# Attention decode backward: scores as 512-column matmuls, and other row splits for nine of the gradient stores

## The chip, the cores and the metric

The kernel runs on one core of a Trainium2 chip. The metric is device time in microseconds (us) of one launch, as the median of several executions. Lower is better.

## The reference

One query row attends to 8192 keys for each of 2 x 32 = 64 heads, and the gradients of q, k and v are wanted as well as the output. All tensors are bf16.

```python
B, H, Sq, Sk, D = 2, 32, 1, 8192, 128

def _fwd_reference(q, k, v):
    scale = q.shape[-1] ** -0.5
    scores = jnp.einsum("bhqd,bhkd->bhqk", q, k) * scale
    p = _softmax(scores, axis=-1)
    return jnp.einsum("bhqk,bhkd->bhqd", p, v)

def reference(q, k, v, grad_out):
    _out, _vjp = jax.vjp(_f, q, k, v)      # _f is _fwd_reference
    return (_out, *_vjp(grad_out))         # out, dq, dk, dv
```

For one head this is: s = K q; p = softmax(s * scale); out = p V; dp = V g (g is the row of grad_out); dS = p * (dp - sum(p * dp)) * scale; dq = dS K; dk = dS times q as an outer product; dv = p times g as an outer product. Each head reads 2 MB of K and 2 MB of V and writes 2 MB of dk and 2 MB of dv, so 537 MB cross between device memory and the core in one launch.

## The kernel before

A head's K and V are each one tile `kvt` of 128 partitions x 64 rows x 128 columns: partition p holds the 64 consecutive keys from 64p on, which are 16 KB in one piece in memory. There are twelve such tiles (`NTILE`), used in turn. dk is written over K in its tile and dv over V, and the tile is stored from there. The tile of a new head is thus free only when the store of the old gradient has landed.

The program is one loop over slots `g`. A slot takes one chunk of 16 key rows per partition; a head has eight slots, four for K (w = 0) and four for V (w = 1). `at(r0)` and `within(r0)` pick the head that has reached a given slot of its own schedule, so a head's later stages stand beside the first stages of the next heads. `pin` keeps every instruction in program order on its engine. The stages of a head are:

- `load` (L98): DMAs issued by SP, six heads ahead. SP works in order and waits until the tile's last store has landed.
- `transpose_chunk`: 16 TensorE transposes into `tp` (L184), copied by ScalarE to `ev` (L186).
- `score_chunk` (L195), one slot later: 16 matmuls, each with a 128x128 block of `ev` as weights and q (or g) as the one moving column. The scores land in the layout [partition, key row], in `sw` for K and `dpw` for V.
- `max_part`, `max_all`, `max_spread`, `expo`: VectorE's row maximum (L207), a maximum over the partitions by way of TensorE (L211, L218), ScalarE's exponential (L238), and the weights `E_pad` (L247) for the matmuls with V.
- `normalise_p`, `weigh`, `normalise_ds`: sums over partitions by fp32 matmuls with ones (L282), then `dS_pad` and the factors `pair` of the outer products.
- `acc` (L339): out and dq, as matmuls with 64 weight columns and 512 moving columns, in two column groups of TensorE; `pick` and `join` (L356, L362, L376) take the wanted blocks out of them.
- `broadcast` (L168, L177): q or g on all partitions.
- `outer` (L394): VectorE writes dk or dv over the tile, and the last chunk's store is issued: by GpSimd (L412), or for the last head in four pieces by SP.

Eight dk stores, those of the heads in `SPREAD`, are cut by `by_rows` (L87) into a DMA of 126 partitions and one of 2. At the start q's first `FIRST` = 6 rows come by a GpSimd DMA (L110) after a reset of that queue's cursor, and the other 58 by SP (L114).

```python
FIRST = 6
SPREAD = range(4, 60, 7)
...
            if w == 0 and i in SPREAD:
                by_rows(store_eng, dst, h.tile[w], (P - 2, 2))
```

Of the kernel before, what the change touches and what calls it, by code (L numbers as in the profile page):

```python
# [11 lines left out]
BF16 = mybir.dt.bfloat16  # L12
F32 = mybir.dt.float32

CH = 16
QT = 4
CW = 64
NG = 2
NTILE = 12
FIRST = 6  # L20
SPREAD = range(4, 60, 7)


@with_exitstack
def kernel(
# [50 lines left out]
    heads = [Head() for _ in range(BH)]  # L76

    def slot_of(i, w):

        n = 2 * i + w  # L80
        return n if n < NTILE else slot_of(i - NTILE // 2, 1 - w)

    def by_rows(eng, dst, src, rows):

        p = 0
        for m in rows:
            pin(eng.dma_start(out=dst[p : p + m], in_=src[p : p + m], max_dma_last_dim=NT * D))  # L87
            p += m

    def load(i, w, pieces=(NCH,)):  # L90
        h = heads[i]
        t = kvp.tile([P, NT, D], BF16, tag=f"kv{slot_of(i, w)}", name="kvt")
        h.tile[w] = t
        src = (v_v if w else k_v)[i]
        c = 0
        for m in pieces:
            n0, n1 = c * CH, (c + m) * CH
            pin(load_eng.dma_start(out=t[:, n0:n1, :], in_=src[:, n0:n1, :]))  # L98
            c += m
# [4 lines left out]
    for w, a in enumerate((q, grad_out)):  # L104
        rows = a.rearrange("b h s d -> (b h s) d")
        r0 = FIRST if w == 0 else 0
        if r0:
# [3 lines left out]
                    out=qd_nat[:r0, w, :], in_=rows[:r0], max_dma_last_dim=D  # L111
# [4 lines left out]
    load(0, 1)  # L116
    for j in range(1, min(NTILE // 2, BH)):
        load(j, 0)
# [17 lines left out]
    nc.vector.memset(E_pad[:], 0.0)  # L136
    nc.vector.memset(dS_pad[:], 0.0)

    qdT = const.tile([P, 2, BH], BF16)
    for w in range(2):  # L140
        tps = ps_m.tile([P, BH], BF16, tag=f"acc{w}", name="tps")
        nc.tensor.transpose(tps[:], qd_nat[:BH, w, :], ident_bf[:BH, :BH])
        nc.vector.tensor_copy(out=qdT[:, w, :], in_=tps[:])

    dqT = const.tile([P, BH], BF16)
    oT = const.tile([P, BH], BF16)

    def begin_s(i):

        h = heads[i]  # L150
        sw = ps_sdp.tile([P, NT + P + 1], F32, tag="s", name="sw")
        h.s = sw[:, 0:NT]
        h.mT = sw[0:1, NT : NT + P]
        h.mb = sw[:, NT + P :]

    def begin_dp(i):

        h = heads[i]
        dpw = ps_sdp.tile([P, NT + 2 + D], F32, tag="dp", name="dpw")
        h.dp = dpw[:, 0:NT]  # L160
        h.lsum = dpw[:, NT : NT + 2]
        h.qbp = dpw[:, NT + 2 :]

    def broadcast(i, w):

        h = heads[i]
        pin(
            nc.tensor.matmul(  # L168
                h.qbp,
                lhsT=qdT[:, w, i : i + 1].to_broadcast([P, P]),  # L170
                rhs=ident_bf[:],
                start=True,
                stop=True,
            )
        )
        h.qb[w] = small.tile([P, D], BF16, tag=f"qb{w}", name="qb")
        pin(nc.vector.tensor_copy(out=h.qb[w][:], in_=h.qbp))  # L177
# [9 lines left out]
        return ev  # L187

    def score_chunk(i, c, ev):
        h = heads[i]  # L190
        w, c = divmod(c, NCH)
        dst = h.dp if w else h.s
        for t in range(CH):
            pin(
                nc.tensor.matmul(  # L195
                    dst[:, c * CH + t : c * CH + t + 1],
                    lhsT=ev[:, t, :],
                    rhs=qdT[:, w, i : i + 1],
                    start=True,
                    stop=True,  # L200
                )
            )
# [125 lines left out]
    def acc(i, w, c):  # L328
# [59 lines left out]
    def outer(i, w, c, ends):  # L388

        h = heads[i]  # L390
        n0 = c * CH
        shape = [P, CH, D // 2, 2]
        pin(
            nc.vector.tensor_tensor(  # L394
                out=h.tile[w][:, n0 : n0 + CH, :].rearrange("p n (e t) -> p n e t", t=2),
                in0=h.qb[w][:]
                .rearrange("p (e t) -> p e t", t=2)
                .unsqueeze(1)
                .to_broadcast(shape),
                in1=h.pair[w][:, n0 : n0 + CH, :].unsqueeze(2).to_broadcast(shape),  # L400
                op=ALU.mult,
            )
        )
        if c + 1 in ends:
            at = ends.index(c + 1)
            b0, b1 = (ends[at - 1] if at else 0) * CH, (c + 1) * CH
            dst = (dv_v if w else dk_v)[i]
            if w == 0 and i in SPREAD:
                by_rows(store_eng, dst, h.tile[w], (P - 2, 2))
            else:  # L410
                eng = load_eng if len(ends) > 1 else store_eng
                pin(eng.dma_start(out=dst[:, b0:b1, :], in_=h.tile[w][:, b0:b1, :]))  # L412
# [6 lines left out]
    last = list(range(1, NCH + 1))  # L419
    AHEAD = NTILE // 2  # L420

    prev = None
    for g in range(SL * BH + O0 + NCH + 4 - SL):
        now = [(g // SL - b, g % SL + b * SL) for b in range(4)]
        now = [(i, r) for i, r in now if 0 <= i < BH]

        def at(r0):

            return next((i for i, r in now if r == r0), None)

# [12 lines left out]
        ev = None  # L443
        if g < SL * BH:
            i, r = divmod(g, SL)
            if r == 0:
                begin_s(i)
            if r == 3:
                begin_dp(i)
                broadcast(i, 1)  # L450
            if r == 6:
                broadcast(i, 0)
            ev = transpose_chunk(i, r)
        if (i := at(A1 + NCH + 2)) is not None:
            join(i, 1)
        if (i := at(A0 + NCH + 2)) is not None:
            join(i, 0)
        if x := within(A1):
            acc(x[0], 1, x[1])
        if x := within(A0):  # L460
            acc(x[0], 0, x[1])
        if (i := at(NCH + 2)) is not None:
            max_spread(i)
            expo(i)
        if prev is not None:
            score_chunk(*prev)
        prev = (g // SL, g % SL, ev) if ev is not None else None

        if (i := at(NCH)) is not None:
            max_part(i)  # L470
        if (i := at(NCH + 1)) is not None:
            max_all(i)
        if (i := at(NCH + 3)) is not None:
            normalise_p(i)
        if (i := at(SL)) is not None:
            weigh(i)
        if (i := at(SL + 1)) is not None:
            normalise_ds(i)
        if (i := at(A1 + NCH)) is not None:
            pick(i, 1)  # L480
        if (i := at(A0 + NCH)) is not None:
            pick(i, 0)

    for w, (src, dst) in enumerate(((dqT, out_1), (oT, out_0))):
        tps = ps_m.tile([BH, P], BF16, tag=f"acc{w}", name="tps")
# [34 lines left out]
```

## Time and profile before

| what | value |
|---|---|
| median of 12 runs | 1286.44 us (1284.68 to 1289.83) |
| the profiled execution, its own time | 1287.36 us |
| its span, first to last instruction | 1285.6 us |
| TensorE busy / its weight loads | 1128.3 us (88%) / 857.9 us |
| VectorE, ScalarE, GpSimd busy | 935.7, 975.1, 76.0 us |
| mean granted TensorE clock | 0.955 |
| DMA: bytes, mean rate | 539.68 MB, 420 GB/s |
| DMA: share of 16 engines' span | 49.9% SP's queue, 48.7% GpSimd's queue, 0.7% instruction fetch |

The span is what the profile sees; 1287.36 - 1285.6 = 1.8 us lie around it. "Share of 16 engines' span" says how long the packets of a queue took, summed over the 16 DMA engines of the core. A compute engine's busy time overlaps the others', and matmuls are pipelined, so a busy share is not a share of the work. A launch spans 64 heads, so one head has 1285.6 / 64 = 20.1 us, and one slot 2.51 us.

### The profile page before, as it was taken

The numbers are of one execution on the slowest core, as the hardware profiler recorded it, in microseconds if no ns is written. First come the engines' busy times: TensorE is split into PE (matmuls) and PEld (weight loads), VectorE is DVE, ScalarE is ACT, GpSimd is POOL, SyncE is SP. The second block draws the span as 40 slices with busy tenths as digits, with TensorE's granted clock in tenths as the row PEclk, the third lists the DMA queues.
The fourth block names the chain that finished last, engine by engine and source line by source line (L and its number), as shares of the span: only waits on it lengthen the run. The fifth ranks groups of instructions, "written<-read, shape, count | busy, mean of one in ns | idle before, by whom it ended". The sixth has DMA issues, their size and how long they took to land.

```text
span 1285.6 us, 42576 instructions
## 1 busy us (share of the span) xinstructions
PE 1128.3 (88%) x19268; PEld 857.9 (67%) x19268; DVE 935.7 (73%) x2122; ACT 975.1 (76%) x641; POOL 76.0 (6%) x143
## 2 busy tenths in 40 slices
PE   6999999999989988997889799897989789889881
PEld 5777777667666766776666576675767666667650
DVE  2888888778777867686777677775777677777772
ACT  6888888878777877786777678786778677777750
POOL 0000000000000000000000000000000000000000
PEclk9999999999998989898999999998989899999995
DMA  9999999999999999999999999999999999999995
GB/s 387 424 426 426 428 427 426 428 426 426 427 429 425 421 427 428 426 420 426 428 427 423 426 427 428 423 423 427 429 425 426 421 428 427 426 424 428 428 398 244
DMA packets 40194, 539.68 MB, mean 420 GB/s; under 512 B 5196, under 2 KB 5196, under 8 KB 6476
## 3 DMA queue, kind: packets, MB, share of 16 engines
q1 hardware_dynamic: 20172, 272.70, 49.9%
q0 software_dynamic: 19840, 264.25, 48.7%
q8 instruction: 150, 2.46, 0.7%
q14 instruction: 32, 0.26, 0.0%
HBM read 268.47 MB, written 268.47 MB: 418 GB/s over the span
## 4 chain that ended last, share of the span: by engine, by line
DMA 35%; another core or an unknown queue 22%; PE 22%; DVE 11%; issue 6%; ACT 2%; SPq 1%; POOL 0%; POOLq 0%; DVEq 0%; ACTq 0%
DMA kvt<-in_v_dram 27%; PE tp L184 10%; DVE kvt L394 6%; PE acc L339 5%; DMA kvt<-in_k_dram 5%; DMA out_dram<-kvt 3%; PE dpw L195 3%; PE sw L195 2%; DVE sel L362 2%; ACT ev L186 1%; SPq L98 1%; DVE sel L356 1%; PE dpw L282 1%; DMA qd_nat<-in_q_dram 1%
## 5 line engine op out<-in xcount | busy, mean ns | idle before, releaser
L186 ACT COPY ev<-tp 128x2048 bf16<-128x2048 bf16 x512 | 954.3, 1865 | 270.3 <-PE tp L184 258.8
L184 PE MATMUL tp<-ident_bf,kvt 128*128 128x128 bf16 x8192 | 557.6, 223 | 99.1 <-DMA kvt<-in_v_dram 83.9
L394 DVE TENSOR_TENSOR kvt<-qb,pair 128x2048 bf16<-128x2048 bf16 x512 | 621.6, 1215 | 0.2
L184 PEld LDWEIGHTS <-kvt 128*128 128x128 bf16 x8192 | 489.1, 100 | 105.7 <-DMA kvt<-in_v_dram 87.5
L195 PEld LDWEIGHTS <-ev 128*128 128x128 bf16 x8192 | 243.1, 96 | 208.9 <-issue 150.8
L339 PE MATMUL acc<-kvt,dS_pad 128*64 128x512 bf16 x1024 | 168.5, 412 | 0.8 <-DVE dqT L379 0.8
L339 PE MATMUL acc<-kvt,E_pad 128*64 128x512 bf16 x1024 | 160.1, 393 | 0.0
L195 PE MATMUL dpw<-qdT,ev 128*128 128x1 bf16 x4096 | 140.6, 164 | 17.9 <-DVE qb L177 17.0
L362 DVE SCALAR_TENSOR_TENSOR sel<-acc,diag,sel 128x128 f32<-128x128 f32 x384 | 134.7, 351 | 13.6
L195 PE MATMUL sw<-qdT,ev 128*128 128x1 bf16 x4096 | 141.9, 164 | 1.1 <-ACT ev L186 1.1
L207 DVE TENSOR_REDUCE mp<-sw 128x1 f32<-128x64 f32 x64 | 14.4, 225 | 163.8 <-PE sw L195 163.8
L412 POOL DMA_DIRECT2D out_dram<-kvt x118 | 63.3, 536 | 1085.7 <-DVE kvt L394 899.2
L339 PEld LDWEIGHTS <-dS_pad 128*64 128x64 bf16 x1024 | 37.7, 111 | 24.7 <-issue 5.7
L247 DVE CAST E_pad<-E_f 128x64 bf16<-128x64 f32 x64 | 12.5, 196 | 55.3 <-ACT E_f L238 55.3
L339 PEld LDWEIGHTS <-E_pad 128*64 128x64 bf16 x1024 | 36.4, 108 | 21.2 <-issue 0.5
L376 PE MATMUL acc<-ones,sel 128*128 128x1 f32 x256 | 43.5, 239 | 6.2 <-DVE sel L362 6.2
L282 PE MATMUL dpw<-ld,ones 128*128 128x1 f32 x256 | 46.3, 250 | 0.1
L376 PEld LDWEIGHTS acc<-ones,sel 128*128 128x128 f32 x256 | 39.3, 194 | 7.3 <-DVE sel L362 7.3
L356 DVE TENSOR_SCALAR sel<-acc,diag 128x128 f32<-128x128 f32 x128 | 44.1, 344 | 0.0
L253 DVE CUSTOM_DVE_ANT_0 junk<-E_f,dpw 128x64 bf16<-128x64 f32 x64 | 14.1, 221 | 37.0 <-PE dpw L195 37.0
L177 DVE CAST qb<-dpw 128x128 bf16<-128x128 f32 x128 | 35.5, 278 | 6.0 <-PE dpw L168 6.0
L282 PEld LDWEIGHTS dpw<-ld,ones 128*128 128x128 f32 x256 | 38.2, 188 | 0.5 <-DVE ld L253 0.5
(44 smaller groups left out, 314.6 us busy)
## 6 DMA issues: line engine op xcount, KB each, us to landing
out_dram<-kvt POOLq DMA_DIRECT2D x118, 2048.0 KB, 67.3
kvt<-in_v_dram SPq DMA_DIRECT2D x64, 2048.0 KB, 20.2
kvt<-in_k_dram SPq DMA_DIRECT2D x63, 2048.0 KB, 20.3
out_dram<-kvt POOLq DMA_DIRECT2D x8, 2016.0 KB, 73.1
out_dram<-kvt SPq DMA_DIRECT2D x8, 512.0 KB, 23.0
kvt<-in_k_dram SPq DMA_DIRECT2D x2, 512.0 KB, 4.5
kvt<-in_k_dram SPq DMA_DIRECT2D x1, 1024.0 KB, 7.1
out_dram<-kvt POOLq DMA_DIRECT2D x8, 32.0 KB, 72.6
```

The lines of the kernel that those rows point to most:

```text
L177: pin(nc.vector.tensor_copy(out=h.qb[w][:], in_=h.qbp))
L184: pin(nc.tensor.transpose(tp[:, t, :], src[:, c * CH + t, :], ident_bf[:]))
L186: pin(nc.scalar.copy(out=ev[:], in_=tp[:]))
L195: nc.tensor.matmul(dst[:, c * CH + t : c * CH + t + 1], lhsT=ev[:, t, :], rhs=qdT[:, w, i : i + 1], start=True, stop=True,)
L207: pin(nc.vector.reduce_max(out=h.mp[:], in_=h.s, axis=AX.X))
L282: nc.tensor.matmul(out, lhsT=ones[:].to_broadcast([P, P]), rhs=col, start=True, stop=True)
L339: nc.tensor.matmul(h.acc[w][g : g + CW, :], lhsT=wts[:, n0 : n0 + CW], rhs=rows[:, n0 : n0 + QT, :].rearrange("p n d -> p (n d)"), start=( ...
L356: nc.vector.tensor_scalar(out=h.sel[:], in0=block, scalar1=diag[:, 0:1], scalar2=None, op0=ALU.mult)
L362: nc.vector.scalar_tensor_tensor(out=h.sel[:], in0=block, scalar=diag[:, b : b + 1], in1=h.sel[:], op0=ALU.mult, op1=ALU.add,)
L376: nc.tensor.matmul(h.acc[w][:, 0:1], lhsT=h.sel[:], rhs=ones[:], start=True, stop=True)
L394: nc.vector.tensor_tensor(out=h.tile[w][:, n0 : n0 + CH, :].rearrange("p n (e t) -> p n e t", t=2), in0=h.qb[w][:] .rearrange("p (e t) -> ...
L412: pin(eng.dma_start(out=dst[:, b0:b1, :], in_=h.tile[w][:, b0:b1, :]))
```

## The change

**Scores.** q and g are kept transposed in a row of zeros, one value in every fourth column (`qdT`, now 291 columns for each). A window of 32 columns that begins c columns before head i's value (the row starts with three zero columns for this) has q in its column c, and no other head's value in columns 0 to 3. With the window as weights, a chunk's scores are four matmuls of 512 moving columns (four key rows x 128 partitions), one in each of four 32-wide column groups. The four chunks add into one PSUM tile `raw`: row 32g + c holds the scores of chunk c, group g. `keep_raw` copies it to SBUF (`rows`, 128x512 fp32), and `spread_rows` brings it to the old layout by four fp32 matmuls with a one-hot right-hand side (`sel4`, 16 columns). This is done once for K and once for V of each head. `max_part`, `max_all`, `max_spread` with `expo`, `normalise_p`, `weigh` and `normalise_ds` stand one slot later than before; `acc`, `outer`, loads and stores stay in their slots. s, dp and the small results now share one PSUM bank, and `raw` has another.

**Stores.** The eight stores of 126 + 2 partitions are gone. Seven dk stores (heads in `ONE`) go as 120 partitions by GpSimd and 7 by SP; the last partition's 16 KB go as two small GpSimd DMAs (9 and 8 pieces of 256 B; 3 and 2 for head 52) and the rest by SP. Two (heads in `TWO`) go as 112 + 2 partitions by GpSimd and 7 + 7 by SP. `FIRST` is 5.

```diff
-FIRST = 6
-SPREAD = range(4, 60, 7)
+SG = 4
+SW = 32
+FIRST = 5
+ONE = {4: 9, 12: 9, 20: 9, 28: 9, 36: 9, 44: 9, 52: 3}
+TWO = (57, 61)
...
+    sel4 = const.tile([P, NCH, SG], F32)
+    nc.vector.memset(sel4[:], 0.0)
+    for g in range(SG):
+        nc.vector.tensor_copy(
+            out=sel4[g * SW : (g + 1) * SW, :, g],
+            in_=ident_f[g * SW : (g + 1) * SW, g * SW : g * SW + NCH],
+        )
+
+    Q0 = NCH - 1
+    qdT = const.tile([P, 2, Q0 + NCH * BH + SW], BF16)
...
     def score_chunk(i, c, ev):
         h = heads[i]
         w, c = divmod(c, NCH)
-        dst = h.dp if w else h.s
-        for t in range(CH):
+        if c == 0:
+            h.raw = ps_sdp.tile([P, QT * P], F32, tag="raw", name="raw")
+        q0 = Q0 + NCH * i - c
+        for g in range(SG):
             pin(
                 nc.tensor.matmul(
-                    dst[:, c * CH + t : c * CH + t + 1],
-                    lhsT=ev[:, t, :],
-                    rhs=qdT[:, w, i : i + 1],
+                    h.raw[g * SW : (g + 1) * SW, :],
+                    lhsT=qdT[:, w, q0 : q0 + SW],
+                    rhs=ev[:, g * QT : (g + 1) * QT, :].rearrange("p n d -> p (n d)"),
+                    start=(c == 0),
+                    stop=(c == NCH - 1),
                 )
             )
+
+    def keep_raw(i):
+        h = heads[i]
+        h.rows = work.tile([P, QT * P], F32, tag="rows", name="rows")
+        pin(nc.vector.tensor_copy(out=h.rows[:], in_=h.raw[:]))
+
+    def spread_rows(i, w):
+        h = heads[i]
+        for t in range(QT):
+            pin(
+                nc.tensor.matmul(
+                    h.score[w].rearrange("p (n t) -> p n t", t=QT)[:, :, t],
+                    lhsT=h.rows[:, t * P : (t + 1) * P],
+                    rhs=sel4[:].rearrange("p c g -> p (c g)"),
                     start=True,
                     stop=True,
                 )
             )
...
-            if w == 0 and i in SPREAD:
-                by_rows(store_eng, dst, h.tile[w], (P - 2, 2))
+            if w == 0 and i in ONE:
+                by_rows(store_eng, dst, h.tile[w], (P - 8,))
+                by_rows(load_eng, dst, h.tile[w], (7,), P - 8)
+                a = 2 * ONE[i]
+                for eng, cols in (
+                    (store_eng, slice(0, a - 1, 2)),
+                    (store_eng, slice(1, a - 2, 2)),
+                    (load_eng, slice(a - 1, NT)),
+                ):
+                    pin(
+                        eng.dma_start(
+                            out=dst[P - 1 :, cols, :], in_=h.tile[w][P - 1 :, cols, :]
+                        )
+                    )
+            elif w == 0 and i in TWO:
+                by_rows(store_eng, dst, h.tile[w], (P - 16, 2))
+                by_rows(load_eng, dst, h.tile[w], (7, 7), P - 14)
...
+        if (i := at(NCH + 1)) is not None:
+            spread_rows(i, 0)
+        if (i := at(SL + 1)) is not None:
+            spread_rows(i, 1)
-        if (i := at(NCH + 2)) is not None:
+        if (i := at(NCH + 3)) is not None:
             max_spread(i)
             expo(i)
         if prev is not None:
             score_chunk(*prev)
...
         if (i := at(NCH)) is not None:
+            keep_raw(i)
+        if (i := at(SL)) is not None:
+            keep_raw(i)
+        if (i := at(NCH + 1)) is not None:
             max_part(i)
```

More of the change, by code (lines that the diff above doesn't have):

```diff
@@ L81, in slot_of, with by_rows @@
         return n if n < NTILE else slot_of(i - NTILE // 2, 1 - w)
-    def by_rows(eng, dst, src, rows):
-        p = 0
+    def by_rows(eng, dst, src, rows, p=0):
         for m in rows:
@@ L137 @@
     nc.vector.memset(dS_pad[:], 0.0)
-    qdT = const.tile([P, 2, BH], BF16)
+    sel4 = const.tile([P, NCH, SG], F32)
[7 more added lines that the diff above has]
+    qdT = const.tile([P, 2, Q0 + NCH * BH + SW], BF16)
+    nc.vector.memset(qdT[:], 0.0)
     for w in range(2):
@@ L142, with begin @@
         nc.tensor.transpose(tps[:], qd_nat[:BH, w, :], ident_bf[:BH, :BH])
-        nc.vector.tensor_copy(out=qdT[:, w, :], in_=tps[:])
+        nc.vector.tensor_copy(
+            out=qdT[:, w, Q0 : Q0 + NCH * BH].rearrange("p (i f) -> p i f", f=NCH)[:, :, 0],
+            in_=tps[:],
+        )
     dqT = const.tile([P, BH], BF16)
     oT = const.tile([P, BH], BF16)
-    def begin_s(i):
+    def begin(i):
         h = heads[i]
[L151 to L162, printed above, removed]
+        sw = ps_sdp.tile([P, 2 * NT + 2 * P + 4], F32, tag="s", name="sw")
+        h.score = (sw[:, 0:NT], sw[:, NT : 2 * NT])
+        h.s, h.dp = h.score
+        h.mT = sw[0:1, 2 * NT : 2 * NT + P]
+        h.qbp = sw[:, 2 * NT + P : 2 * NT + 2 * P]
+        h.lsum = sw[:, 2 * NT + 2 * P : 2 * NT + 2 * P + 2]
+        h.mb = sw[:, 2 * NT + 2 * P + 2 : 2 * NT + 2 * P + 3]
     def broadcast(i, w):
@@ L169, in broadcast @@
                 h.qbp,
-                lhsT=qdT[:, w, i : i + 1].to_broadcast([P, P]),
+                lhsT=qdT[:, w, Q0 + NCH * i : Q0 + NCH * i + 1].to_broadcast([P, P]),
                 rhs=ident_bf[:],
@@ L191, in score_chunk @@
         w, c = divmod(c, NCH)
-        dst = h.dp if w else h.s
-        for t in range(CH):
+        if c == 0:
+            h.raw = ps_sdp.tile([P, QT * P], F32, tag="raw", name="raw")
+        q0 = Q0 + NCH * i - c
+        for g in range(SG):
             pin(
                 nc.tensor.matmul(
-                    dst[:, c * CH + t : c * CH + t + 1],
-                    lhsT=ev[:, t, :],
-                    rhs=qdT[:, w, i : i + 1],
+                    h.raw[g * SW : (g + 1) * SW, :],
[4 more added lines that the diff above has]
+                )
+            )
+    def keep_raw(i):
[10 more added lines that the diff above has]
+                    rhs=sel4[:].rearrange("p c g -> p (c g)"),
                     start=True,
@@ L407, in outer @@
             dst = (dv_v if w else dk_v)[i]
-            if w == 0 and i in SPREAD:
-                by_rows(store_eng, dst, h.tile[w], (P - 2, 2))
+            if w == 0 and i in ONE:
[10 more added lines that the diff above has]
+                            out=dst[P - 1 :, cols, :], in_=h.tile[w][P - 1 :, cols, :]
+                        )
+                    )
+            elif w == 0 and i in TWO:
+                by_rows(store_eng, dst, h.tile[w], (P - 16, 2))
+                by_rows(load_eng, dst, h.tile[w], (7, 7), P - 14)
             else:
@@ L445 @@
             i, r = divmod(g, SL)
[L446 to L449, printed above, removed]
+            if r == NCH:
+                begin(i)
                 broadcast(i, 1)
-            if r == 6:
+            if r == NCH + 2:
                 broadcast(i, 0)
@@ L469 @@
         if (i := at(NCH)) is not None:
+            keep_raw(i)
+        if (i := at(SL)) is not None:
+            keep_raw(i)
+        if (i := at(NCH + 1)) is not None:
             max_part(i)
-        if (i := at(NCH + 1)) is not None:
+        if (i := at(NCH + 2)) is not None:
             max_all(i)
-        if (i := at(NCH + 3)) is not None:
+        if (i := at(NCH + 4)) is not None:
             normalise_p(i)
-        if (i := at(SL)) is not None:
+        if (i := at(SL + 1)) is not None:
             weigh(i)
-        if (i := at(SL + 1)) is not None:
+        if (i := at(SL + 2)) is not None:
             normalise_ds(i)
```

## The prediction

> **What bounds the kernel now.** First the page's slices and DMA queues (shares are of 16 engines' span):
>
> ```profile
> PEclk9999999999998989898999999998989899999995
> DMA  9999999999999999999999999999999999999995
> GB/s 387 424 426 426 428 427 426 428 426 426 427 429 425 421 427 428 426 420 426 428 427 423 426 427 428 423 423 427 429 425 426 421 428 427 426 424 428 428 398 244
> ...
> q1 hardware_dynamic: 20172, 272.70, 49.9%
> q0 software_dynamic: 19840, 264.25, 48.7%
> q8 instruction: 150, 2.46, 0.7%
> ```
>
> The DMA engines are full from the first slice to the last but one, while no compute engine is above 88%. Second, the queue's own waits, and those of TensorE: SP spends nearly the whole span waiting for stores to land before it may load.
>
> ```profile
> SPq L98 <- DMA out_dram<-kvt: 1141.3, 116, 24.3
> ```
>
> ```profile
> PE tp L184 <- DMA kvt<-in_v_dram: 83.9, 42, 6.9
> ```
>
> Third, stages at the end (us, PE, PEld, DVE, ACT, POOL busy, clock, DMA share, GB/s):
>
> ```profile
> 1200.00:1240.00 40.00, 34.23 (x594) 26.01 (x592) 28.76 (x66) 30.08 (x21) 2.13 (x4) 1.00 1.01 427
> 1260.00:1270.00 10.00, 0.90 (x3) 0.63 (x3) 2.31 (x8) 0.00 (x0) 0.00 (x0) 0.50 0.74 304
> 1270.00:1286.00 16.00, 0.00 (x0) 0.00 (x0) 0.00 (x0) 0.00 (x0) 0.00 (x0) 0.50 0.32 130
> ```
>
> All arithmetic is over at 1263.6, yet a part of the DMA engines goes on. So the load of the *busiest DMA engines* sets the end, not the mean load.
>
> Which ones? Packet records name no engine, but a full engine starts each packet 3 or 4 ns before its last one ends, so the records string into 16 chains. A 16 KB packet takes 611 ns. Read so:
> - Instruction fetches (16 KB, 978 ns) go round eight of the 16 engines in a fixed order. From 1020 to 1140 us an engine with two fetches moved 193 packets, a plain one 197.5: a fetch costs 4.5 x 0.611 / 2 = 1.37 us with the delays beside it. 150 / 8 = 18.75 each: 25.7 us.
> - One engine without fetches moved 189, with 153 packets above 611 ns: 8.5 x 0.611 = 5.2 us lost in 120, so some 53 us in the 1225 full ones.
> - At the end seven engines work to 1280.5, the others stop at 1264 to 1274.
>
> **What the Trainium skill says.** "DMA: Bandwidth & Descriptors", section "Why a DMA increments its semaphore by 16 and not by 1": a DMA uses the largest k up to 16 that divides the outer dimension; SP's takes the lowest-numbered engines, GpSimd's k engines in turn from a cursor. The trace agrees for 126 + 2: in three such stores 14 chains hold 54 half-row packets each and two hold 6. With the cursor at 6 after `FIRST` those two are engines 4 and 5. The same page's "Latency and other measured facts" knows slow engines and guesses at GpSimd's descriptor rings; here it is one engine, and one of those two, as the other of them takes fetches. None of engines 0 to 3 (found by the first loads) fetches. Eight neighbours that hold just one of 4 and 5 and none of 0 to 3 can only be 5 to 12. I take that: **fetches on 5 to 12, the slow engine is 4**. That they are neighbours is assumed. "TensorEngine Tiling (Array Packing)", "Key Properties": column tiles work in parallel, and a change of tiling drains the array. The trace agrees for two groups: `acc`'s four matmuls of 512 columns take 0.56 us, whereas 16 transposes of 128 columns take 0.98 from start to start, that is 0.25 per 512 columns and 0.98 for four in series.
>
> **Part 1, the stores and fetches on the DMA engines.** TensorE loses 8192 weight loads and 8192 matmuls; it gains 2048 of each for the scores, and 512 fp32 matmuls of four instructions (L282's 128 show as 256 + 256): 16384 - 4096 - 2048 = 10240 fewer. VectorE gains 128. 150 fetches for 42576 instructions are 284 each, and with the 19 fetches' worth of early 8 KB packets 252; at 256, 10112 / 256 = 40 fewer. 110 / 8 = 13.8 each x 1.37 = 18.9 us.
>
> Rows relative to eight on every engine, x 0.611 us. Before, a 126 + 2 store gives 14 engines +1 and two -7, eight times. After, a `ONE` store gives engine 4 -8 (cursor 5, 15 engines) and engines 0 to 6 +1 from SP's 7 rows; a `TWO` store gives all -1, 0 to 6 +2, and two of 9 to 12 +1. The 256 B pieces take 18 ns, nothing, and bring the cursor back to 5; the 12 KB rest adds at most 0.45 x 7 = 3 us to engine 0, which has room.
>
> | engines | before | after |
> |---|---|---|
> | 0-3 | +8 rows: 4.9 us | +9: 5.5 |
> | 4 (slow) | -56, +53: 18.8 | -47, +53: 24.3 |
> | 5 | -56, +25.7: -8.5 | +9, +18.9: 24.4 |
> | 6 | +8, +25.7: 30.6 | +9, +18.9: 24.4 |
> | 7-12 | +8, +25.7: 30.6 | -2 or -1, +18.9: 17.7 to 18.3 |
> | 13-15 | +8: 4.9 | -2: -1.2 |
>
> The check on before: seven engines at 30.6, just the number that works to 1280.5; engine 4 is 11.8 behind that, 1268.7, where chains do end. The busiest goes from 30.6 to 24.4: **-6.2 us**. Bounds: a fetch at 1.3 and 44 fewer, or 36 fewer, give -5.5 to -7; engine 4 at 57 instead of 53 leaves -2.3.
>
> **Part 2, TensorE.** Its time is free as long as it keeps up with the loads. A head without long waits:
>
> ```profile
> 701.57 1.05 PE L184 MATMUL tp<-ident_bf,kvt 128*128 128x128 bf16 x16
> 702.55 0.62 PE L339 MATMUL acc<-kvt,dS_pad 128*64 128x512 bf16 x4
> 703.11 0.55 PE L195 MATMUL dpw<-qdT,ev 128*128 128x1 bf16 x16
> 703.52 0.36 PE L282 MATMUL dpw<-ld,ones 128*128 128x1 f32 x2
> 703.79 1.07 PE L184 MATMUL tp<-ident_bf,kvt 128*128 128x128 bf16 x16
> ```
>
> From start to start: transposes 0.98, `acc` 0.56, scores 0.41, an fp32 matmul 0.22 to 0.27. The same stage of the next head starts at 718.95: 17.4 us. Loads let TensorE have (1245 - 14) / 64 = 19.2 us for each head (start at 14, last V chunk by 1245). New scores per slot: in series 0.98; two at a time as `acc` 0.56; four at a time one pass of 0.25 plus the rest of `acc`'s 0.56 - 2 x 0.25 = 0.06, so 0.31 at least, and I take 0.34 for one more change of tiling. That is 8 x (0.34 - 0.41) = -0.6. Spreads: 8 x 0.22 = 1.8 (0.8 if they pipeline, 2.2 at most). Sum 17.4 - 0.6 + 1.8 = 18.6: under 19.2 but close, so worth nothing on the sum. The drop of scores' weight loads is worth nothing either: loads hide it.
>
> **Part 3, what waits anew.** `keep_raw` is 128x512 fp32; from L247 (64 columns, 196 ns) and L177 (128, 278 ns) it is 278 + 384 x 1.28 = 770 ns (at most four of L362's 351), x128 = 99 us: VectorE 936 to 1035 of 1286, or 1116 at most. Behind it wait `pick` and the next `outer`; `spread_rows` waits for it, but stands 1.5 us later behind transposes and `acc`. ScalarE's `expo` one slot later: `E_pad` was ready 0.65 us into the next slot, and `acc` needs it 1.0 us into it. Free, by 0.3 us. If covers fail, a stall of 0.3 us per head is 20 us of TensorE time, against 64 x 0.6 = 38 of slack.
>
> SP's share of a cut store stands behind the load that waits for dv of the same head, and then behind that load's 2 MB in the queue (20 us to landing), so the next load leaves up to 10 us later, nine times. GpSimd's queue has 67 us of stores to go on with, so the engines stay full; TensorE waits 10 us and catches up at 20.1 - 18.6 = 1.5 us per head, in 7 of the 8 heads between two such stores. Free, or a few us; the last load may land at 1240 instead of 1236, and compute then ends at 1267, before the busiest engines' 1274. GpSimd issues 8 more DMAs of 0.5 us, and idles. The q load on one engine (59 x 18 ns, +0.5 us) delays only a start that DMA covers.
>
> **Sum.** 1287.4 - 6.2 = 1281.2 against the profiled execution; the median is 0.9 lower: **1280.5**.
>
> **Rivals.** (A) As above: 1278 to 1284; chance 0.65. (B) TensorE becomes the bound: column groups work two at a time, as the only such row in the profile does. 17.4 + 1.2 + 1.8 = 20.4 per head, 14 + 64 x 20.4 + 40 of tail = 1360; it decides from 19.2 per head, scores at 0.41 per slot with these spreads, and near that point it costs 1284 to 1300. A lower granted clock does the same. For it: the margin of 0.6. Against: `acc` already runs its two groups beside each other. 0.15. (C) The slow engine is 5, or fetches lie elsewhere: engine 5 is at 5.5 + 53 = 58.5, +28 us, 1314. 0.06. (D) The balance is gained and lost again, by late loads at nine stores or engine 4 slower than read: 1284 to 1289, no change. 0.14.
>
> Faster by over 0.2% (2.6 us, about what a measurement here tells from no change): A without its upper edge, 0.64. Within: D and edges, 0.14. Slower: B, C, 0.22. The range 1276 to 1294 holds A, D and B's near end and leaves out 0.2.
>
> **What would show it.** Right: instruction packets near 110; fewer engines at work after the last arithmetic; TensorE's wait for loads still there; SP still waiting for stores. Wrong: TensorE's waits for loads gone and DMA slices below 9 (B); one engine alone at the end for 30 us (C); last V load landing after 1245 (D).

## The result and the profile after

The changed kernel takes **1303.07 us** (median of 8 runs, 1299.88 to 1305.05) where the kernel before takes 1286.5 (median of 32 runs; the first twelve gave 1286.44): a ratio of 1.0123, 95% interval 1.0112 to 1.0135. It was forecast at 1280.5 and is 16.6 us slower than before. The profiled execution has a span of 1299.9 us.

The page of the changed kernel, slices and DMA queues (DMA share in tenths and GB/s for each of 40 slices; then each queue's packets, MB and share of 16 engines):

```profile
DMA  9999999999999999999999999999999999999965
GB/s 391 425 429 428 428 424 427 429 428 427 420 427 430 425 428 418 428 429 428 425 412 431 427 424 425 409 428 429 425 425 426 431 428 427 418 417 427 422 256 208
...
q1 hardware_dynamic: 20417, 274.05, 49.9%
q0 software_dynamic: 19808, 262.90, 47.9%
q8 instruction: 110, 1.80, 0.5%
```

The instruction packets fell from 150 to 110, as forecast. Isolated slices of 409 to 418 GB/s are new (before, none between the first and the last two is under 420), and the last two slices are worse, 256 and 208 where they were 398 and 244. The waits of SP's queue and of TensorE (us in total, times, longest):

```profile
SPq L100 <- DMA out_dram<-kvt: 1133.2, 104, 38.4
```

```profile
PE tp L194 <- DMA kvt<-in_v_dram: 11.7, 6, 6.5
```

SP still waits for stores nearly all the time, but its longest wait has grown from 24.3 to 38.4 us. TensorE hardly waits for V loads any more: 11.7 us instead of 83.9. The end of the span, in stretches (us, PE, PEld, DVE, ACT, POOL busy, clock, DMA share, GB/s):

```profile
1270.00:1280.00 10.00, 7.34 (x36) 3.74 (x34) 9.68 (x24) 0.00 (x0) 0.38 (x1) 0.55 0.90 356
1280.00:1290.00 10.00, 2.79 (x12) 1.12 (x8) 5.67 (x12) 0.00 (x0) 0.00 (x0) 0.50 0.71 285
1290.00:1300.00 10.00, 0.00 (x0) 0.00 (x0) 0.00 (x0) 0.00 (x0) 0.00 (x0) 0.50 0.06 23
```

A DMA share of 0.06 is one engine of sixteen (1 / 16 = 0.0625): for the last ten microseconds a single DMA engine works alone. The chain of waits and SP's timeline show a second new thing shortly before:

```profile
1209.23 30.07 DMA out_dram<-kvt
1239.44 16.03 DMA kvt<-in_v_dram
```

```profile
1208.87 0.68 SPq L89 DMA_DIRECT2D out_dram<-kvt  x2
1239.44 0.36 SPq L100 DMA_DIRECT2D kvt<-in_v_dram  x1
```

SP issues its rows of head 57's store at 1208.87; the next load, the last one, waits 30 us for that store and its data are there only at 1255.5. Before, the last load left at 1216 and landed at 1236.

### The profile page after: what moved, and what is told of

It reads as the page before. It is cut to its first block, busy times and chain, and to the rows that moved or that the text cites. A ratio compares the mean times of both kernels' runs of the same rounds, so it can differ in the third digit from the quotient of the medians.

```text
span 1299.9 us, 32523 instructions
## 1 busy us (share of the span) xinstructions
PE 1196.8 (92%) x14148; PEld 813.3 (63%) x14148; DVE 1026.0 (79%) x2256; ACT 975.3 (75%) x641; POOL 79.5 (6%) x151
## 4 chain that ended last, share of the span: by engine, by line
PE 57%; DVE 15%; DMA 14%; ACT 10%; issue 2%; SPq 0%; ACTq 0%; DVEq 0%
PE tp L194 24%; PE acc L372 14%; DMA kvt<-in_v_dram 9%; PE raw L208 9%; ACT ev L196 8%; DVE kvt L427 6%; DMA out_dram<-kvt 5%; PE sw L228 4%; DVE sel L395 4%; DVE rows L221 3%; PE sw L315 3%; PE sw L178 2%; PE acc L409 1%; ACT E_f L271 1%; DVE sel L389 1%
## 5 line engine op out<-in xcount | busy, mean ns | idle before, releaser
L427 DVE TENSOR_TENSOR kvt<-qb,pair 128x2048 bf16<-128x2048 bf16 x512 | 616.9, 1216 | 0.0
L194 PE MATMUL tp<-ident_bf,kvt 128*128 128x128 bf16 x8192 | 547.5, 220 | 12.2 <-DMA kvt<-in_v_dram 11.7
L208 PE MATMUL raw<-ev,qdT 128*32 128x512 bf16 x2048 | 205.8, 392 | 1.5 <-ACT ev L196 1.5
L372 PE MATMUL acc<-kvt,E_pad 128*64 128x512 bf16 x1024 | 160.2, 393 | 23.8 <-DVE E_pad L280 23.5
L228 PEld LDWEIGHTS sw<-sel,rows 128*128 128x128 f32 x1024 | 124.0, 191 | 52.4 <-DVE sel L395 25.9
L208 PEld LDWEIGHTS <-qdT 128*32 128x32 bf16 x2048 | 53.1, 93 | 137.8 <-issue 132.9
L228 PE MATMUL sw<-sel,rows 128*128 128x16 f32 x1024 | 136.5, 265 | 0.0
L221 DVE COPY rows<-raw 128x512 f32<-128x512 f32 x128 | 88.6, 692 | 38.1 <-PE raw L208 38.1
L178 PE MATMUL sw<-ident_bf,qdT 128*128 128x128 bf16 x128 | 28.5, 223 | 36.2 <-DVE mp L240 36.2
L246 DVE TENSOR_REDUCE gm<-sw 1x1 f32<-1x128 f32 x64 | 17.8, 279 | 55.4 <-PE sw L244 55.4
L315 PEld LDWEIGHTS sw<-ld,ones 128*128 128x128 f32 x256 | 38.1, 188 | 29.7 <-issue 14.8
L315 PE MATMUL sw<-ld,ones 128*128 128x1 f32 x256 | 49.1, 261 | 0.0
```

The costliest lines, as they stand in the source:

```text
L194: pin(nc.tensor.transpose(tp[:, t, :], src[:, c * CH + t, :], ident_bf[:]))
L208: nc.tensor.matmul(h.raw[g * SW : (g + 1) * SW, :], lhsT=qdT[:, w, q0 : q0 + SW], rhs=ev[:, g * QT : (g + 1) * QT, :].rearrange("p n d -> ...
L221: pin(nc.vector.tensor_copy(out=h.rows[:], in_=h.raw[:]))
L228: nc.tensor.matmul(h.score[w].rearrange("p (n t) -> p n t", t=QT)[:, :, t], lhsT=h.rows[:, t * P : (t + 1) * P], rhs=sel4[:].rearrange("p ...
L315: nc.tensor.matmul(out, lhsT=ones[:].to_broadcast([P, P]), rhs=col, start=True, stop=True)
L372: nc.tensor.matmul(h.acc[w][g : g + CW, :], lhsT=wts[:, n0 : n0 + CW], rhs=rows[:, n0 : n0 + QT, :].rearrange("p n d -> p (n d)"), start=( ...
```

## The experiments

Each edit is against the changed kernel unless it says otherwise (x3 and x10 against the kernel before). Each ratio is to the kernel before on the same chip; the chips differ between some of the runs, so differences of 1 or 2 us between runs are not to be relied on. All of them compute the full result.

**Which part costs: x4_scores_only and x3_stores_only.** x4 has the new scores with the eight old 126 + 2 stores and `FIRST = 6`; x3 has the old scores with the new stores.

```diff
# x4_scores_only: stores as before
+FIRST = 6
+SPREAD = range(4, 60, 7)
...
+            if w == 0 and i in SPREAD:
+                by_rows(store_eng, dst, h.tile[w], (P - 2, 2))
```

> The changed scores alone; stores as before (126 + 2 rows eight times, q's first rows 6). Theory L: the last load leaves on time; the fetches on the busiest DMA engines fall from 18.75 to 13.8 each, 1279 to 1285 us. Theory P: 1299 to 1304 us, with TensorE's waits for loads near zero. If TensorE is a bound only in part: 1286 to 1295 us.

> The kernel before with the new stores alone; scores by single-column matmuls as before. Theory L: the last load is 15 to 25 us late here too, 1297 to 1308 us, though TensorE has its old slack. Theory P: 1283 to 1290 us, as only the scores cost time.

x4 measured **1279.89 us**, ratio 0.9946 (0.9931 to 0.9961): 7.3 us faster than the 1287.21 of before on that chip. x3 measured **1317.05 us**, ratio 1.0231 (1.0215 to 1.0246): 30 us slower. So the scores alone gave what was forecast for the whole, and the stores lost it several times over.

**Which part of the stores: x1_no_two, x2_two_late, x6_no_pieces, x5_rows_17.** x1 drops the two `TWO` stores; x2 moves one of them from head 57 to 59, past the last load; x6 drops `TWO` and the 256 B pieces, so that SP takes the last row whole; x5 keeps everything but cuts a `ONE` store into whole rows whose engines add up to 15 + 9 + 8 = 32.

```diff
# x1_no_two, x6_no_pieces: TWO = ();  x2_two_late: TWO = (59, 61)
# x5_rows_17: in place of the 120 rows, the 7 rows and the three pieces
+                by_rows(store_eng, dst, h.tile[w], (P - 23, 9, 8))
+                by_rows(load_eng, dst, h.tile[w], (3, 3), P - 6)
# x6_no_pieces: in place of the 7 rows and the three pieces
+                by_rows(load_eng, dst, h.tile[w], (7, 1), P - 8)
```

> The changed kernel, but the dk stores of heads 57 and 61 go whole, by GpSimd alone. Theory L (the last load was late because SP's 14 rows of head 57's store stood before it): the last V load leaves near 1216 to 1220 us instead of 1239, the kernel takes 1281 to 1287 us. Theory P (TensorE is the bound all along, 19.4 us and more per head): no change, 1299 to 1304 us. Theory N (each of the nine cut stores costs a little, about 2 us): 1299 us.

> The changed kernel, with head 59 in the place of head 57 among the stores of 112 + 2 + 7 + 7 rows: the same rows on the same DMA engines, but no load stands behind SP's part any more. Theory L: 1281 to 1287 us, like the kernel that sends both whole. Theory P and theory N: 1299 to 1304 us.

> The changed kernel, but each of the seven stores of ONE goes as 105 + 9 + 8 whole rows by GpSimd (15, 9 and 8 engines; 32 steps of the cursor, so that each begins at 5 again) and 3 + 3 rows by SP. No small pieces. Theory C (the 256 B pieces did not bring the cursor back, so only the first of the seven stores spared the slow engine): now all seven spare it, 42 rows less; 1278 to 1286 us. Theory S (SP's rows in a load's way cost the time): 1295 to 1303 us, as they still stand there. Theory P (TensorE): 1299 to 1304 us, but the scores alone have spoken against it.

> The changed kernel with the two small GpSimd DMAs of each store in ONE left out: the last row goes whole by SP. Heads 57 and 61 are stored whole. Theory C: the pieces moved the cursor by nothing in all, so it drifts by 15 each time as it did with them; 1297 to 1301 us, the same as the run without TWO, and other engines than the slow one are spared after the first store. If the pieces did bring the cursor back: it drifts only now, and this is 5 us and more slower than the run without TWO, 1304 to 1315 us.

x1: 1299.04 us (ratio 1.0095, 1.0078 to 1.0112); x2: 1302.12 (1.0116, 1.0101 to 1.0131); x6: 1303.58 (1.0124, 1.0091 to 1.0156); x5: **1282.63** (0.9955, 0.994 to 0.9971). The late load at head 57 is worth 1 us at most, which is within the intervals, and both `TWO` stores 4; that is not the loss. Taking the pieces away changes nothing for the better; x6 even lies 4.5 us above x1, which is taken up below the table further down. Rows that bring the cursor round take 20.4 us off the changed kernel, although the `TWO` stores are still there and SP's rows (six now, in the changed kernel seven and most of another) still hold up the loads. After the second of the seven stores, for one, x5's next load leaves 36.5 us after SP's rows:

```profile
290.87 0.66 SPq L89 DMA_DIRECT2D out_dram<-kvt  x2
327.40 0.36 SPq L100 DMA_DIRECT2D kvt<-in_v_dram  x1
```

For the seven stores these gaps are 36 to 42 us in x5 and 28 to 39 us in the changed kernel. The wait of the loads is thus not what costs 20 us.

What differs is which engine is spared. Packets strung into 16 chains, as in the prediction, show it. (Where two chains end a packet at nearly the same nanosecond they can be taken for one another, so a count can be off by a few.) The slow engine is the one chain with many packets 5 to 130 ns too long; a store of 120 rows gives 16 half-row packets to each engine that it uses, and x5's leaves 4 to the spared one:

```
half-row packets of each ONE store on the slow chain (long packets of it / of the next chain)
store     1          2         3         4         5         6         7
after     0 (17/0)   15 (15/5) 16 (19/1) 16 (35/1) 16 (42/2) 16 (66/1) 16 (64/2)
x5        4 (16/5)   4 (19/3)  4 (29/1)  4 (31/2)  4 (30/0)  4 (37/1)  4 (33/0)
```

In the changed kernel only the first of seven stores spares the slow engine; the other six each leave some other chain with none. In x1 it is the same (0, then 16 six times). So each store moves the cursor back by one, 15 engines of 16, and the pieces do not bring it back: the 17 pieces of each of the first six stores lay on nine of the 16 chains, two on each of eight and one on the ninth, so both DMAs began on the same engine, and they moved the cursor by nothing.

**Is the slow engine really 4: x8_first7.** x4 with `FIRST = 7`, so that the eight 126 + 2 stores spare engines 5 and 6.

```diff
# against x4_scores_only
-FIRST = 6
+FIRST = 7
```

> The scores alone with the old stores, and FIRST = 7, so that the eight stores of 126 + 2 rows spare engines 5 and 6 in the place of 4 and 5. If the slow engine is 4: it keeps all its rows and eight more and bounds the kernel, 1304 to 1313 us. If it is 5: no change, 1278 to 1283 us.

1306.49 us (1.0145, 1.0106 to 1.0184), **26.6 us above x4**. The end has the same look as that of the changed kernel, little more than one engine at work for 19 us:

```profile
1290.00:1300.00 10.00, 0.00 (x0) 0.00 (x0) 0.00 (x0) 0.00 (x0) 0.00 (x0) 0.50 0.07 29
1300.00:1309.00 9.00, 0.00 (x0) 0.00 (x0) 0.00 (x0) 0.00 (x0) 0.00 (x0) 0.50 0.05 22
```

The slow engine is 4, as the prediction took it to be, and leaving it unspared costs about as much as the changed kernel's loss against x4.

**What bounds x4: x7_scores_bcast.** In the new score layout TensorE's `broadcast` waits for VectorE, because s, dp and its own result share one PSUM tile. x7 is x4 with `broadcast(i, 0)` one slot later.

```diff
# against x4_scores_only
-            if r == NCH + 2:
+            if r == NCH + 3:
                 broadcast(i, 0)
```

> The scores alone with the old stores, and the broadcast of q one slot later (r == NCH + 3), so that TensorE does not wait for max_part there (38 us in 63 waits). If TensorE has become the second bound beside the DMA engines: 1 to 8 us faster than the scores alone, 1272 to 1279 us. If the busiest DMA engines bound it still: no change, 1278 to 1282 us.

1281.35 us (0.9959, 0.9945 to 0.9972), the same as x4 within the intervals. But the timelines differ. The row of `gm` on VectorE comes once per head; first x4, then x7:

```profile
705.15 0.28 DVE L245 TENSOR_REDUCE gm<-sw 1x1 f32<-1x128 f32 x1 [0.86 <-PE sw L243]
...
724.59 0.28 DVE L245 TENSOR_REDUCE gm<-sw 1x1 f32<-1x128 f32 x1 [0.86 <-PE sw L243]
```

```profile
717.71 0.28 DVE L245 TENSOR_REDUCE gm<-sw 1x1 f32<-1x128 f32 x1 [0.47 <-PE sw L243]
...
737.02 0.28 DVE L245 TENSOR_REDUCE gm<-sw 1x1 f32<-1x128 f32 x1 [0.48 <-PE sw L243]
```

A head takes 19.44 us in x4, regularly, with no wait for loads: TensorE and what it waits for set the pace of its arithmetic. In x7 it is 19.31. The wait has only become shorter: TensorE now waits there for `gm` of the same tile, 0.37 us per head where x4 waits 0.60 for `mp` (38.1 us in all):

```profile
PE sw L177 <- DVE gm L245: 23.7, 64, 0.4
```

Over 64 heads 0.13 us are 8 us, and x7's arithmetic is over at 1262 where x4's ends at 1271. The time did not follow, because in x7 the DMA engines still run on (x4, then x7):

```profile
1260.00:1270.00 10.00, 3.64 (x21) 1.44 (x17) 9.45 (x15) 0.00 (x0) 0.00 (x0) 0.67 0.98 400
1270.00:1280.00 10.00, 0.62 (x3) 0.34 (x3) 0.57 (x3) 0.00 (x0) 0.00 (x0) 0.50 0.26 102
```

```profile
1260.00:1270.00 10.00, 0.90 (x3) 0.63 (x3) 0.87 (x4) 0.00 (x0) 0.00 (x0) 0.50 0.63 261
1270.00:1280.00 10.00, 0.00 (x0) 0.00 (x0) 0.00 (x0) 0.00 (x0) 0.00 (x0) 0.50 0.22 87
```

So x4 has two bounds within a few microseconds of each other, the busiest DMA engines, as x7 shows, and the pace of the arithmetic. That the second would hold if the DMA engines were faster is argued from its regular heads; no run shows it.

**What the stores would be worth: x10_stores_17, x9_balanced.** x10 has the old scores with x5's stores. x9 has the new scores and fifteen cut stores meant to spare the fetching engines in turn and then engine 4.

```diff
# x9_balanced, against the changed kernel; FIRST = 15
+            if w == 0 and i in SPREAD:                   # last seven
+                by_rows(store_eng, dst, h.tile[w], (P - 2, 2))
+            elif w == 0 and i in ONES:                   # first six and the eighth
+                by_rows(store_eng, dst, h.tile[w], (P - 8,))
+                by_rows(load_eng, dst, h.tile[w], (4, 4), P - 8)
+            elif w == 0 and i in SHIFT:                  # the seventh
+                by_rows(store_eng, dst, h.tile[w], (14, P - 16))
+                by_rows(load_eng, dst, h.tile[w], (2,), P - 2)
```

> The scores as in the kernel before, and the stores as x5_rows_17 cuts them: 105 + 9 + 8 whole rows by GpSimd and 3 + 3 by SP for the seven heads of ONE, the two stores of TWO as in the changed kernel. It says what the stores part is worth when its cursor comes back as it was meant to: fetches stay at 150, 25.7 us on each of eight engines with at most one row above the mean, engine 4 some 40 rows below it with 50 us lost, about 25. The busiest engine of before was 30.6 by the same table. Theory C (the stores' loss of 30 us in x3 is the cursor alone): 1281 to 1288, that is 0 to 5 us below before. Theory S (SP's extra rows before its loads, or the number of small DMAs, cost by themselves): above 1290.

> The scores part as in the changed kernel, and fifteen dk stores cut on purpose by the cursor rule of x5: FIRST = 15; seven stores as 120 rows by GpSimd and 4 + 4 by SP (the 15-engine DMA moves the cursor back by one each time, so that the spared engines are 14, 13, 12, 11, 10, 9, and, after one store of 14 + 112 rows and 2 by SP, which moves the cursor to 7, engine 6), then seven of 126 + 2 that spare 4 and 5. Rows relative to eight per engine: engines 6 and 9 to 14 end at -1 with 18.9 us of fetches, 18.3 us; engine 4 at -49 with about 48 us lost to its slowness, some 18; 0 to 3 at 12.8; the rest below. The busiest was 23.8 us by the same table in x4_scores_only. Theory R (whole rows go to engines by the cursor rule, fetches go round 5, 6, 9 to 14, the busiest DMA engine sets the end, and TensorE still has room at 19.4 us per head): 5.5 us below x4, 1272 to 1279. Rival T (with the scores made this way TensorE or its waits are as near as the DMA engines, so better balance brings nothing): 1279 to 1285, as x4. Rival W (the set of fetching engines is read wrongly, or SP's rows before its loads cost): above 1285.

x10: 1288.02 us, ratio 1.0005 (0.9994 to 1.0016), at the upper edge of its range: no change. It lies 29 us below x3, which has the old scores too and the pieces in place of whole rows, so the cursor is worth as much there as in x5. The forecast had engine 4 lose 50 us to its slowness; counted as for the table further down it lost 58.2, which makes it the busiest engine and gives 1288.8 for a span of 1286.1. Its last load also left late, at 1232.31, after 45 us behind SP's rows of head 57; that was not tried apart. x9: **1289.39 us**, ratio 1.0018 (1.0005 to 1.0032), 10 to 17 us above what the row table gave. Its stores did spare what they were to spare (the seven `ONES` a chain that is not the slow one, the last seven stores the slow one). One part of the miss is engine 4 again: it lost 57 us instead of the 48 of the forecast, so with 49 rows fewer it stands at 27 us and not at 18, and by the table the span ends at 1282 and not at 1273. It ended at 1288.7. SP's own waits and its timeline show another part:

```profile
SPq L102 <- DMA out_dram<-kvt: 1105.2, 80, 58.2
```

```profile
300.57 0.37 SPq L102 DMA_DIRECT2D kvt<-in_v_dram  x1
...
306.05 1.07 SPq L102 DMA_DIRECT2D kvt<-in_v_dram  x1
```

SP waits up to 58.2 us (before: 24.3). Its rows lie in its queue behind the loads that it issued earlier; the next load needs the tile that these rows leave. When they have landed, the queue is empty, and SP issues five loads in 6 us. The queues in the 10 us before that burst, and the stretches around it:

```profile
q0 software_dynamic: 244, 3.59, 84.3%
q1 hardware_dynamic: 50, 0.42, 9.9%
```

```profile
280.00:290.00 10.00, 10.00 (x129) 6.99 (x128) 9.12 (x22) 7.82 (x5) 1.06 (x2) 1.00 1.01 432
290.00:300.00 10.00, 9.04 (x107) 6.16 (x107) 7.41 (x16) 7.89 (x7) 0.30 (x1) 1.00 0.95 402
300.00:310.00 10.00, 10.00 (x124) 6.58 (x121) 9.05 (x24) 7.88 (x5) 0.77 (x2) 1.00 0.97 378
310.00:320.00 10.00, 9.04 (x112) 6.47 (x112) 7.44 (x17) 7.35 (x6) 0.75 (x1) 1.00 0.99 399
```

SP's queue has run dry (9.9% where it normally has half), and for 30 us the engines move 402, 378 and 399 GB/s instead of some 428. Only about half of that is idleness. The DMA share is 0.95 and 0.97 and 0.99, so from 300 on the engines are nearly full again and still move 378 and 399: their packets take longer. Summed over the eight stores with rows by SP, about 4 MB are missing, 9 us. How the miss of x9 divides between engine 4, the dry queue and the longer packets is not shown. A long wait need not cost: x5, with up to 42 us behind rows, has no slice between the first and the last two under 421 GB/s. So although the slices of 409 to 418 GB/s in the changed kernel stand where SP's rows held up the next load, the wait alone does not explain them; x4, without such rows, has one of 413.

**A finer balance without SP: x11_bcast_split, x12_split.** Twelve stores cut into whole rows for GpSimd alone, with x7's scores and with x4's.

```diff
# against x7_scores_bcast (x11) and x4_scores_only (x12)
+FIRST = 5
+SPLIT = (
+    (105, 3, 20), (4, 120, 4), (5, 18, 105), (120, 8), (105, 5, 18), (12, 105, 11),
+    (6, 120, 2), (15, 105, 8), (5, 18, 105), (12, 105, 11), (8, 105, 15), (120, 8),
+)
+SPREAD = range(2, 60, 5)
...
+                by_rows(store_eng, dst, h.tile[w], SPLIT[SPREAD.index(i)])
```

> x7_scores_bcast with its eight 126 + 2 stores replaced by twelve dk stores (heads 2 to 57, every fifth) that are cut into two or three pieces of whole rows, all issued by GpSimd, FIRST = 5. By the cursor rule nine of them spare engine 4 and one each 5, 11, 9 or 6, and the row table has the busiest engines at 21.3 us where x7's has 23.8. No row goes by SP, so no load stands behind rows. Reading of x4, x7 and x9: x4 has two bounds within 2 us of each other, the compute chain (19.44 us per head, arithmetic over at 1271) and the DMA engines; x7 moved the first (19.32 us, arithmetic over at 1262) and so is bound by the second alone. Then this kernel gains what the table says: 2.5 us below x7's 1281.3, 1277 to 1280. Rival: the table is too fine to build on, or the compute chain still sets the end: 1280 to 1284.

> The same twelve stores with the scores of x4_scores_only, that is with broadcast(i, 0) one slot earlier again, so that the compute chain has 19.44 us per head. If x4 is bound by compute, its better table brings at most the few tenths that the last stores land sooner: 1279 to 1281, arithmetic over near 1271, and no TensorE wait for loads. If the DMA engines alone bound x4: 2.5 us below it, 1276.5 to 1278.5.

1294.79 us (1.0066, 1.0054 to 1.0078) and 1295.04 (1.0063, 1.0043 to 1.0083): every forecast missed, by 10 us and more. It is not the balance alone. By the cursor rule engine 4 has 47 rows fewer in x11, and it lost 55.1 us, so by the table it would end at 1281.4, and the span ends at 1293.0. The packets of x11 take 1283.4 us per engine in all, those of x7 1275.0, for the same bytes and 110 fetches in both. Packets that are 130 ns or more too long make 16.0 us per engine in x11 and 8.8 in x7. Of these, 11.4 and 4.3 lie in stretches of 5 us in which a cut store is under way; x11 has 115 such stretches and x7 68. Why packets lengthen there, those of the cut stores and those beside them, stays open.

## Why the prediction was wrong, step by step

**The step that failed** is the sentence on the pieces, that they "bring the cursor back to 5". On it rests engine 4's line of the row table: 47 rows fewer, 24.3 us. Only the first `ONE` store took rows from that engine, so its line is -8 + 7 + 2 = +1 row (the 7 are SP's rows of the `ONE` stores, the 2 what the `TWO` stores add), 48 above the -47 of the table; without `TWO` it is -1. These 48 rows are 29.3 us. In this kernel engine 4 lost 44.6 us to its slowness and not 53, so it stands at 24.3 + 29.3 - 8.4 = 45.2 where the busiest engines of before stood at 30.6: 14.6 us more, and the span grew by 14.3. That the loss was 8.4 us smaller is luck; it hid a part of the mistake. With the cursor brought round by whole rows (x5) the kernel takes 1282.63, inside the 1278 to 1284 of rival A. The Trainium skill had a sentence that fits: "DMA: Bandwidth & Descriptors", section "Why a DMA increments its semaphore by 16 and not by 1", names an exception in which GpSimd's DMA counts as one over all 16 engines, with as many engines carrying data as there are shares. The page counts these shares in partitions; here they would be pieces of one partition. Read so, the 9 and 8 pieces agree with it: nine chains, cursor unmoved. The prediction used the rule and passed over its exception. That the piece DMAs are such a case is read from where they landed; no run here tells what makes a DMA one.

The corrected table accounts for the times of these kernels within 3 us. The mean engine of before is 1285.6 - 30.6 = 1255.0 us of span. Add for engine 4 its rows x 0.611 and its loss (16 KB packets 5 to 130 ns too long between 40 and 1200 us, scaled by 1225 / 1160). The loss is counted in the very profile whose span is to be met, so this is an account and not a forecast. In all of them engine 4 is the busiest by the table; it is so in x9, x11 and x12 too, but these end 6 to 12 us above such a sum, for which the runs above give only a part of the reasons:

| kernel | engine 4: rows | loss, us | 1255.0 + both | span |
|---|---|---|---|---|
| changed | +1 | 44.6 | 1300.2 | 1299.9 |
| x1_no_two | -1 | 43.6 | 1298.0 | 1297.0 |
| x2_two_late | +1 | 42.3 | 1297.9 | 1300.6 |
| x6_no_pieces | -1 | 48.6 | 1303.0 | 1302.0 |
| x8_first7 | +8 | 49.8 | 1309.7 | 1309.2 |
| x3_stores_only | +1 | 56.6 | 1312.2 | 1314.5 |
| x10_stores_17 | -40 | 58.2 | 1288.8 | 1286.1 |

The loss of engine 4 itself varies from 42 to 58 us between profiles, also on one chip (42 to 48 in x1, x2 and x4, 57 in x3), and why stays open. In the profile of before it is 57.5 by this count, where the prediction had read 53 from 120 us. By the table, 5 us more of it make x6 slower than x1, but x6 does not end with one engine alone. Its last V load left at 1210.45, and TensorE could begin on it only at 1268.22, 58 us later (in x1 30 us, 1219.8 to 1250.2). Its arithmetic runs to 1297.6, and the last head is stored beside it up to the end, by all engines (the DMA share from 1290 to 1295 is 0.99):

```profile
1284.19 11.08 SPq L449 DMA_DIRECT2D out_dram<-kvt  x8
1297.88 1.13 SPq L532 DMA_DIRECT2D out_dram<-nat  x2
```

So in x6 the late load and the arithmetic behind it end last, together with engine 4 or in its place; which of them sets the time was not tried apart.

**Part 1, scores.** Right. 110 fetches, and x4's 7.3 us against the 6.8 that the table gives with the old stores (the 6.2 of the sum is for the new ones); the busiest engines in x4 are those with fetches, 18.9 + 4.9 = 23.8, so 1278.8 against a span of 1280.4. "Neighbours 5 to 12" was probably wrong and did no harm: start-up packets and the pieces' places speak for 5, 6 and 9 to 14, of which 5 and 6 and none of 0 to 4 are what the table needed.

**Part 2, TensorE.** One head on TensorE's timeline of the changed kernel (start, us, what, wait ahead of it):

```profile
701.99 0.22 PE L178 MATMUL sw<-ident_bf,qdT 128*128 128x128 bf16 x1 [0.60 <-DVE mp L240]
...
706.03 0.40 PE L208 MATMUL raw<-ev,qdT 128*32 128x512 bf16 x4
706.36 1.07 PE L194 MATMUL tp<-ident_bf,kvt 128*128 128x128 bf16 x16
...
719.43 1.07 PE L228 MATMUL sw<-sel,rows 128*128 128x16 f32 x8
720.42 0.40 PE L208 MATMUL raw<-ev,qdT 128*32 128x512 bf16 x4
721.43 0.22 PE L178 MATMUL sw<-ident_bf,qdT 128*128 128x128 bf16 x1 [0.61 <-DVE mp L240]
```

Each size was near. The four `raw` matmuls take 0.33 us from start to start (0.34 forecast): that column tiles work in parallel, as "TensorEngine Tiling (Array Packing)", "Key Properties", says, is now seen for four. The four fp32 matmuls of `spread_rows` take 0.99 (0.88). The sum was not near: 721.43 - 701.99 = 19.44 us per head against 18.6, over the 19.2 that was allowed. It left out two waits (us in total, times, longest):

```profile
PE sw L178 <- DVE mp L240: 36.2, 60, 0.6
...
PE acc L372 <- DVE E_pad L280: 23.5, 62, 1.4
```

The first is the shared PSUM tile, 0.60 us for each head, not seen at all; the second is the `E_pad` called "free, by 0.3 us", 0.38 for each. Together they are 0.98. The 17.4 of before held a wait of 0.32 for `qb` that is gone, so 0.66 of the missing 0.84 are waits, and the two spreads of a head, 0.11 each above their forecast, are 0.22 more; that is the whole gap within 0.04. So "worth nothing on the sum" held only because the DMA engines end at nearly the same time, as x7 showed.

**Part 3.** `keep_raw` 692 ns (770 forecast), VectorE 1026 us (1035): right. "The next load leaves up to 10 us later" was undersized: 28 to 39 us in the changed kernel, as SP's rows stand behind more than one load; x5's 36 to 42 show that this costs little. The last load was to land by 1240 to 1245 and landed at 1255.5; with engine 4 behind anyway, both `TWO` stores cost 4 us (x1). The sum's last step is off by a little, 1281.2 - 0.9 being 1280.3 and not 1280.5.

**The rivals.** None named the cause. The end looks as rival C said, one engine alone, but through the stores' rows and not through a wrong number. D named late loads or a slower engine 4, but as a gain lost again, 1284 to 1289. B's mark of 19.2 us per head was passed, and x4, which has the same 19.44, was still faster than before. Three of the signs of being wrong came at least in part: TensorE's waits for loads nearly gone (B), one engine alone at the end, for 10 us (C), and the last V load at 1255.5 (D). None of them points to the cursor.

## What to carry to other kernels

When the load of single DMA engines sets the end, check in the trace on which engine the second and third of a series of cut stores land, since a cursor that is off by one shows only there; here the first was right and cost nothing, and the next six cost 20 us. Rows of a store in the queue that issues the loads land behind the loads issued earlier and hold up the load that needs their tile, so price that wait by the queue's backlog; here 36 to 42 us of it did no visible harm (x5), and 52 us left SP's queue nearly dry (x9). And when a stage is priced as hidden, list every new shared buffer and the wait that it makes, as well as the instructions.

## What was unexpected of the hardware

- Cutting stores had a price of its own here: with the same bytes, the packets of the kernel with twelve stores cut by rows took 8.4 us more per engine than with eight of 126 + 2 (x11 against x7).
- DMAs of 9 and 8 pieces of 256 B from GpSimd used nine engines in each store and left the cursor, whereas a DMA of 120 whole rows moved it by 15, and DMAs of 105, 9 and 8 whole rows together brought it round to where it was (x5).
- An engine that is 4% slow (about 8.5 rows of 197.5 in 120 us) is worth 26.6 us to this kernel if it is not spared (x8 against x4).
